# Sums of weights on VectorE instead of GpSimd, and a last product in three parts, in an attention and mixer kernel

## The chip, the cores and the metric

The kernel runs on one core of one Trainium2 chip. The metric is device time in microseconds (us) of one execution; lower is better. A few executions are more than 1.5% above the fastest of their kernel and count as slow. A profile is one execution, and its span (first to last instruction) is 1.7 to 2.0 us shorter than the device time of the same run.

In lines of the profile PE is TensorE (matrix products), PEld its loading of weights, DVE VectorE, ACT ScalarE, POOL GpSimd, and PEclk the clock granted to TensorE, in tenths. A line in order of time gives start and length in us, engine, line of the kernel, operation, output<-input, their sizes and a count; a bracket holds the engine's idle time before it and what ended that. SBUF is the on-chip memory of the tiles; TensorE writes its products to banks of another memory, PSUM.

## The reference, cut to what matters

```python
# attention, 8 batches x 8 heads x 576 positions x 64, causal, with a bias
scores = q @ k.T / 8 + minimum(bias, 0);  attn = softmax(masked scores);  x = attn @ v
# mixer on x (8 x 576 x 512)
u  = x + ((x.T @ U) @ V).T                       # low rank, along the positions
out = u + maximum(u @ w_ch1, 0) @ w_ch2          # 512 -> 2048 -> 512
```

Only the last product, hidden times `w_ch2`, matters for the change. The kernel works through the mixer in nine groups of 512 rows, as "fill" between the steps of attention. For the groups after the first it forms this product from a 2x2 block scheme with seven block products instead of eight. That scheme needs sums and differences of the blocks of `w_ch2`: B_1 = B12 - B11, B_2 = B22 - B_1, B_4 = B21 - B_2, and B_3 = B22 - B12, which takes the place of B12.

## The kernel before

The sums of the weights are made by GpSimd, three of them in one series as soon as the loads are issued, the fourth when the first group has stopped using B12:

```python
def weight_sums():
    for dst, a, b in ((B_1, B12, B11), (B_2, B22, B_1), (B_4, B21, B_2)):
        for k2 in range(0, HF, 2):                      # HF = 8
            at = (slice(None), slice(k2, k2 + 2))       # 128 x 512, bf16
            nc.gpsimd.tensor_sub(dst[at], a[at], b[at])
...
load(2); load_v(2)
weight_sums()
...
def chanmix(g, ...):
    if g > 0:
        if g == 1:                                      # fourth sum, in place
            for k2 in range(0, HF, 2): nc.gpsimd.tensor_sub(B_3[at], B22[at], B12[at])
    for nf in range(done, NF):                          # 16 chunks
        f1 = pwork(); hidden(f1, u, nf, range(4))       # TensorE
        nc.scalar.activation(hT[:, nf, :], f1, RELU)    # ScalarE
        ...
```

The causal mask of the probabilities is a VectorE instruction with two inputs in SBUF, and it stands in VectorE's queue ahead of the normalisation that frees the product banks of TensorE:

```python
nc.vector.tensor_tensor(dst, dst, keep[...].to_broadcast(...), op=ALU.min)     # mask
...
nc.vector.reciprocal(rec, po[:, :, D:D+1])                                      # values()
nc.vector.tensor_tensor(x_sb[...], po[:, :, 0:D], rec.to_broadcast(...), op=ALU.mult)
```

The end of each group, after the seventh product p7:

```python
add(U2, U2, p7); add(o22, o22, p7); send(o22, 1, 1)
p4 = bank()
for i in halves:
    product(p4, A22, B_4, i)                            # 8 matmuls 128x256 each
    if i == 0: o21 = quarter(); add_u(o21, U2, 1, 0)    # o21 = U2 + u
add(o21, o21, p4); send(o21, 1, 0)                      # 256 KB
```

The softmax here doesn't subtract the row's maximum and nothing guards it: scores larger than these inputs give would overflow.

## Time and profile before

| | kernel before |
|---|---|
| device time, three runs | 379.25, 381.78, 388.65 us (the last is slow) |
| span of the profiled run | 379.6 us |
| TensorE busy, mean granted clock | 354.7 us (93%), 0.982 |
| VectorE, ScalarE, GpSimd busy | 271.4, 204.6, 101.5 us |
| twelve GpSimd subtractions | 54.4 to 67.7 us |
| longest mask on VectorE | 12.96 us |
| longest idle time of TensorE | 12.15 us |

TensorE is the bound, so a microsecond in which it is idle or at a lower clock is a microsecond of the span, and busy time of the other engines counts only where TensorE waits for it.

### The profile page before, as it was taken

How to read it: one execution, taken by the hardware profiler on the slowest of the kernel's cores; microseconds unless marked ns; L12 is line 12 of the kernel's file. 1: busy time of each engine (PE TensorE's matmuls, PEld its weight loads, DVE VectorE, ACT ScalarE, POOL GpSimd, SP SyncE). 2: the span in 40 equal slices, each digit the busy share in tenths (PEclk: the TensorE clock that was granted, in tenths of full speed). 3: DMA queues.
4: the chain of work that ended last, by engine and by line, in shares of the span. 5: the costliest groups of instructions: out<-in, count | busy, mean ns of one | idle time of the engine just before them, and what ended most of it. 6: DMA issues, size and time to landing. Idle time of an engine off the chain costs nothing.

```text
span 379.6 us, 9369 instructions
## 1 busy us (share of the span) xinstructions
PE 354.7 (93%) x3907; PEld 249.2 (66%) x3951; DVE 271.4 (72%) x565; ACT 204.6 (54%) x309; POOL 101.5 (27%) x124
## 2 busy tenths in 40 slices
PE   7999990799999999999999999999999999999995
PEld 3675650566658866787578766886688568468474
DVE  8775779577769875898489947995698269166075
ACT  3875960275676368816881588148825550540630
POOL 8997459644404040404040404000000000000000
PEclk9999995699999999999999999999999999999999
DMA  7999999998996999799997999454012501502302
GB/s 105 168 200 205 174 178 48 60 157 109 91 106 47 112 133 140 62 74 124 139 97 75 112 151 119 53 94 100 20 38 61 124 17 57 112 2 89 79 28 85
DMA packets 147490, 37.40 MB, mean 99 GB/s; under 512 B 130616, under 2 KB 145816, under 8 KB 147448
## 3 DMA queue, kind: packets, MB, share of 16 engines
q0 software_dynamic: 104640, 18.49, 67.7%
q1 hardware_dynamic: 42808, 18.31, 25.8%
q8 instruction: 31, 0.51, 0.6%
q14 instruction: 11, 0.09, 0.1%
HBM read 37.25 MB, written 9.70 MB: 124 GB/s over the span
## 4 chain that ended last, share of the span: by engine, by line
PE 75%; DVE 12%; ACT 5%; issue 3%; DMA 3%; SPq 0%; POOL 0%; DVEq 0%; ACTq 0%; POOLq 0%
PE pwork L643 28%; PE pwork L688 20%; PE pscore L397 9%; PE pwork L457 7%; DVE hT L342 4%; PE pwork L310 3%; PE pwork L653 3%; ACT hT L789 2%; DVE uT L511 2%; DVE o_sb L702 2%; ACT pT L412 2%; DVE slot L670 2%; DMA slot<-hT 2%; DMA k_sd<-in_k_dram 1%; PE pscore L643 1%
## 5 line engine op out<-in xcount | busy, mean ns | idle before, releaser
L643 PE MATMUL pwork<-uT,w_sb 128*128 128x512 bf16 x525 | 133.6, 379 | 2.4 <-ACT hT L789 0.5
L789 ACT ACTIVATE hT<-pwork 128x512 bf16<-128x512 f32 x140 | 84.2, 605 | 61.3 <-PE pwork L643 61.1
L412 ACT ACTIVATE pT<-pscore 128x1024 bf16<-128x1024 f32 x56 | 57.1, 1029 | 69.5 <-PE pscore L397 63.7
L643 PEld LDWEIGHTS <-w_sb 128*128 128x128 bf16 x576 | 50.7, 98 | 50.0 <-issue 0.9
L397 PE MATMUL pscore<-slot 68*128 68x320 bf16 (+1 forms) x500 | 56.5, 247 | 1.0 <-DMA slot<-hT 0.8
L397 PEld LDWEIGHTS <-slot 68*128 68x128 bf16 x564 | 41.6, 98 | 18.0 <-issue 1.8
L688 PEld LDWEIGHTS <-hT 128*128 128x128 bf16 x512 | 47.7, 98 | 7.7 <-issue 0.7
L185 POOL DMA_DIRECT2D v_slot<-in_v_dram x36 | 30.3, 857 | 83.5 <-PE pwork L457 77.6
L457 PE MATMUL pwork<-v_slot,pT 128*128 128x65 bf16 x870 | 36.1, 195 | 12.4 <-DVE x_sb L467 12.1
L688 PE MATMUL pwork<-w_sb,hT 128*128 128x256 bf16 x384 | 47.5, 273 | 0.0
L342 DVE TENSOR_TENSOR pT<-pT,keep 128x512 bf16<-128x512 bf16 (+1 forms) x81 | 29.7, 366 | 22.8 <-ACT pT L412 15.9
L457 PEld LDWEIGHTS <-pT 128*128 128x128 bf16 x870 | 33.0, 99 | 17.8 <-DVE x_sb L467 12.4
L330 DVE COPY slot<-pwork 64x576 bf16<-64x576 bf16 x70 | 31.7, 453 | 4.7 <-PE pwork L310 4.1
L333 DVE COPY slot<-pwork 64x576 bf16<-64x576 bf16 x35 | 28.1, 803 | 6.1 <-PE pwork L310 4.2
L688 PE MATMUL pwork<-w_sum,slot 128*128 128x256 bf16 x256 | 31.5, 272 | 0.8 <-DVE o_sb L702 0.7
L467 DVE TENSOR_TENSOR x_sb<-pwork,rec 128x320 bf16<-128x320 f32 x64 | 31.2, 489 | 1.4
L423 ACT ACTIVATE pT<-pscore 128x1024 bf16<-128x1024 f32 x29 | 30.2, 1041 | 2.7 <-PE pscore L397 2.4
L466 DVE RECIPROCAL rec<-pwork 128x5 f32<-128x5 f32 x64 | 12.1, 190 | 23.5 <-PE pwork L457 23.2
L670 DVE TENSOR_TENSOR slot<-hT 128x1024 bf16<-128x1024 bf16 x16 | 11.0, 688 | 24.5 <-ACT hT L789 24.3
L688 PEld LDWEIGHTS <-slot 128*128 128x128 bf16 x256 | 24.1, 98 | 4.5 <-issue 1.6
L702 DVE TENSOR_TENSOR o_sb<-o_sb,pwork 128x512 f32<-128x512 f32 x32 | 21.8, 680 | 1.0 <-PE pwork L688 0.3
L111 POOL DMA_DIRECT2D q_sd<-in_q_dram x5 | 11.3, 2250 | 38.9 <-PE pwork L310 38.9
(126 smaller groups left out, 438.2 us busy)
## 6 DMA issues: line engine op xcount, KB each, us to landing
out_dram<-o_sb SPq DMA_DIRECT2D x36, 256.0 KB
w_sb<-in_moe_w_ch_dram POOLq DMA_DIRECT2D x4, 1024.0 KB, 12.4
v_slot<-in_v_dram POOLq DMA_DIRECT2D x28, 128.0 KB, 6.1
q_sd<-in_q_dram POOLq DMA_DIRECT2D x5, 576.0 KB, 12.7
k_sd<-in_k_dram POOLq DMA_DIRECT2D x5, 576.0 KB, 16.5
q_sd<-in_q_dram POOLq DMA_DIRECT2D x4, 288.0 KB, 12.4
k_sd<-in_k_dram POOLq DMA_DIRECT2D x4, 288.0 KB, 11.8
q_sd<-in_q_dram POOLq DMA_DIRECT2D x4, 144.0 KB, 5.1
```

The source lines that it names most:

```text
L185: nc.gpsimd.dma_start(out=vt[:rows_t, t, :, 0:D], in_=v[b, :, ds(t * 128, rows_t), :].rearrange("h p d -> p h d"),)
L330: copies(n, hh, par)(by_run[:, :, :, par, :], src)
L342: nc.vector.tensor_tensor(dst, dst, keep[:, :, 0:w].to_broadcast([128, n_tiles, w]), op=ALU.min)
L397: nc.tensor.matmul(dst, lhsT=slot[0:KA, hh, ds(S + j * 128, 128)], rhs=slot[0:KA, hh, lo:hi], start=True, stop=True,)
L412: nc.scalar.activation(pT[:, hh, 0:1024], near, EXP, scale=scale)
L423: nc.scalar.activation(pT[:, :, 1024:1536], mid.rearrange("p (a b) -> p a b", a=2), EXP, scale=scale)
L457: nc.tensor.matmul(po[:, i, :], lhsT=pT[:, hh, ds(place(j, i), 128)], rhs=vt[:, j, h, :], start=(j == 0), stop=(j == i), skip_group_check= ...
L467: nc.vector.tensor_tensor(x_sb[:, hp, :, ds(hh * D, D)], po[:, :, 0:D], rec.to_broadcast([128, 5, D]), op=ALU.mult,)
L643: nc.tensor.matmul(f1, lhsT=w1_sb[:, kt, ds(nf * 128, 128)], rhs=u[:, kt, :], start=(kt == 0), stop=(kt == 3),)
L688: nc.tensor.matmul(acc[:, i, :], lhsT=a[:, kt, ds(i * 128, 128)], rhs=b[:, kt, :], start=(i == 0 and kt == 0), stop=(kt == HF - 1), skip_g ...
L702: nc.vector.tensor_tensor(dst, a, b, op=ALU.add)
L789: nc.scalar.activation(hT[:, nf, :], f1, RELU)
```

## The change

Its intent is to make the sums on VectorE, in small pieces between the chunks of the second group, when GpSimd's series no longer stands in anything's way, and to let the last product of the last group leave in smaller parts. The diff, cut to its core:

```diff
     def weight_sums():
-        for dst, a, b in ((B_1, B12, B11), (B_2, B22, B_1), (B_4, B21, B_2)):
-            for k2 in range(0, HF, 2):
-                at = (slice(None), slice(k2, k2 + 2))
-                nc.gpsimd.tensor_sub(dst[at], a[at], b[at])
+        for dst, a, b in (..., (B_3, B22, B12)):
+            for k4 in range(0, HF, 4):                   # 128 x 1024
+                ...
+                nc.vector.tensor_sub(dst[at], a[at], b[at])
+                in_program_order(tc, before, [E.DVE])
+                yield
 # end of the last group
+        if g == NG - 1:
+            o21 = quarter(); add_u(o21, U2, 1, 0)
+            for i, lo, hi in ((0, 0, HD), (1, 0, 128), (1, 128, HD)):
+                ...                                      # 8 matmuls of width hi - lo
+                add(o21[:, i, lo:hi], o21[:, i, lo:hi], p4[:, 0, lo:hi])
+                (nc.sync if lo == 128 else nc.scalar).dma_start(...)
+            return
 # second group: the loop over k2 on GpSimd for B_3 goes, and
+            sums = weight_sums() if g == 1 else iter(())
             nc.scalar.activation(hT[:, nf, :], f1, RELU)
+            if g > 0:
+                next(sums, None)
 ...
     load_v(2)
-    weight_sums()
```

More of the change, by code (lines that the diff above doesn't have):

```diff
@@ L250, in weight_sums @@
     def weight_sums():
-        for dst, a, b in ((B_1, B12, B11), (B_2, B22, B_1), (B_4, B21, B_2)):
-            for k2 in range(0, HF, 2):
-                at = (slice(None), slice(k2, k2 + 2))
-                nc.gpsimd.tensor_sub(dst[at], a[at], b[at])
+        for dst, a, b in ((B_1, B12, B11), (B_2, B22, B_1), (B_4, B21, B_2), (B_3, B22, B12)):
+            for k4 in range(0, HF, 4):
+                at = (slice(None), slice(k4, k4 + 4))
+                traced = nc.cur_bb.bb.instructions
+                before = max(i for i, ins in enumerate(traced) if ins.engine == E.DVE)
+                nc.vector.tensor_sub(dst[at], a[at], b[at])
+                in_program_order(tc, before, [E.DVE])
+                yield
     nc.gpsimd.dma_start(
@@ L709, in add_u, with send @@
             )
-        def send(o, r, c, rows=slice(0, 2)):
-            n = rows.stop - rows.start
+        def send(o, r, c):
             nc.sync.dma_start(
-                out=out_flat[
-                    ds(g * 512 + r * 256 + rows.start * 128, n * 128), ds(c * HD, HD)
-                ].rearrange("(i p) d -> p i d", p=128),
-                in_=o[:, rows, :],
+                out=out_flat[ds(g * 512 + r * 256, 256), ds(c * HD, HD)].rearrange(
+                    "(i p) d -> p i d", p=128
+                ),
+                in_=o,
             )
@@ L766, in outputs_by_quarters @@
         send(o22, 1, 1)
+        if g == NG - 1:
+            o21 = quarter()
+            add_u(o21, U2, 1, 0)
+            for i, lo, hi in ((0, 0, HD), (1, 0, 128), (1, 128, HD)):
+                p4 = bank()
+                for kt in range(HF):
+                    nc.tensor.matmul(
+                        p4[:, 0, lo:hi],
+                        lhsT=A22[:, kt, ds(i * 128, 128)],
+                        rhs=B_4[:, kt, lo:hi],
+                        start=(kt == 0),
+                        stop=(kt == HF - 1),
+                    )
+                add(o21[:, i, lo:hi], o21[:, i, lo:hi], p4[:, 0, lo:hi])
+                (nc.sync if lo == 128 else nc.scalar).dma_start(
+                    out=out_flat[ds(g * 512 + 256 + i * 128, 128), lo:hi], in_=o21[:, i, lo:hi]
+                )
+            return
         p4 = bank()
@@ L781, in chanmix @@
             hT = work.tile([128, NF, 512], BF16, tag="hT", name="hT")
-            if g == 1:
-                for k2 in range(0, HF, 2):
-                    at = (slice(None), slice(k2, k2 + 2))
-                    nc.gpsimd.tensor_sub(B_3[at], B22[at], B12[at])
+            sums = weight_sums() if g == 1 else iter(())
         for nf in range(done, NF):
```

## The prediction

> **What bounds the kernel now.** I read the page first, for the shape of the span in 40 slices (9.5 us each):
>
> ```profile
> PE   7999990799999999999999999999999999999995
> DVE  8775779577769875898489947995698269166075
> POOL 8997459644404040404040404000000000000000
> PEclk9999995699999999999999999999999999999999
> ```
>
> TensorE is the bound almost everywhere (93% of the span busy), with one hole: slice 6, from 57 to 66 us, where its digit is 0 and from where its granted clock falls to 0.5 and 0.6. So I asked for the chain of waits in order of time around this hole, then for the busy times by stretch, then for GpSimd and VectorE in order of time.
>
> ```profile
> 53.32 0.81 DVE slot L333
> 54.13 0.01 issue
> 54.14 0.81 DVE slot L333
> 54.95 12.86 DVE hT L342
> 67.81 0.03 issue
> 67.84 0.21 DVE rec L466
> ```
>
> The chain's columns are start, length and what ran. It sits for 12.86 us in a single VectorE instruction at line 342, a causal mask of 128x128 bf16. The table of line 342 gives the masks on pT a range of 196 to 1229 ns, and those on hT a largest of 12956 ns. GpSimd in order of time shows what else ran then (start us, length us, engine, line, operation, how many):
>
> ```profile
> 54.38 4.48 POOL L254 TENSOR_TENSOR w_sum<-w_sb 128x512 bf16<-128x512 bf16 x4
> 58.83 8.90 POOL L254 TENSOR_TENSOR w_sum<-w_sb,w_sum 128x512 bf16<-128x512 bf16 x8
> ```
>
> VectorE over the same time, in order:
>
> ```profile
> 54.85 12.96 DVE L342 TENSOR_TENSOR hT<-hT,keep 128x128 bf16<-128x128 bf16 x1
> 67.84 0.20 DVE L466 RECIPROCAL rec<-pwork 128x5 f32<-128x5 f32 x1
> ```
>
> The twelve subtractions of the weight sums run without a gap from 54.38 to about 67.7 us (1.14 us each), and the mask that began 0.47 us after the first of them ends 0.1 us after the last. Everything behind it on VectorE waits, and TensorE with it, since its product banks are freed by the normalisation at line 467:
>
> ```profile
> 55.87 0.61 PE L397 MATMUL pscore<-slot 68*128 68x128 bf16 x6
> 68.62 1.01 PE L457 MATMUL pwork<-v_slot,pT 128*128 128x65 bf16 x15 [12.15 <-DVE x_sb L467]
> 69.84 1.49 PE L653 MATMUL pwork<-w_sb,hT 128*128 128x512 bf16 x3 [0.22 <-issue]
> ```
>
> The bracket says that TensorE was idle 12.15 us. By stretch (length; busy us of TensorE, weight load, VectorE, ScalarE, GpSimd; clock; DMA):
>
> ```profile
> 58.00:68.00 10.00, 0.00 (x0) 0.00 (x0) 9.97 (x2) 0.00 (x0) 10.00 (x10) 0.54 0.92 30
> 68.00:72.00 4.00, 3.16 (x25) 2.07 (x27) 2.14 (x7) 0.00 (x0) 4.00 (x2) 0.50 0.41 24
> 72.00:76.00 4.00, 3.94 (x64) 2.96 (x64) 2.07 (x7) 2.33 (x3) 0.15 (x1) 0.94 1.98 120
> ```
>
> After the hole TensorE goes on at half clock until about 72.3 us, then at full clock.
>
> **What the Trainium skill says.** (1) "SBUF — State Buffer", section "Who interferes with whom": a VectorE instruction with two SBUF inputs contends with a GpSimd instruction that reads SBUF, and the one that comes second blocks. The trace agrees in kind: the mask (two SBUF inputs) stood, while copies from PSUM beside the later GpSimd subtractions at 87.9 to 92.4 us kept their usual time (0.68 us for 128x512). The page speaks of holding the port "for the whole instruction"; here the mask was held over all twelve (13.0 us, not 1.1). (2) "TensorE: Matmul & The Clock Gate", section "What's actually happening": the clock halves after an idle window of about 3.4 us and recovers after a busy one. The trace agrees: 0.50 in the hole, and full again some 3.7 us after work resumed. (3) "GPSIMD Engine Reference", section "4.1 Engine selection": elementwise work with two inputs belongs on VectorE, GpSimd being about twice as slow. The trace: 1.14 us for 128x512 bf16 on GpSimd against 0.69 us for twice as much (128x1024, line 670) on VectorE.
>
> **The change part by part.**
> *Removed: the twelve GpSimd subtractions at 54 us.* TensorE's idle 12.15 us goes. Without the port being held the mask takes 0.2 us, and two reciprocals and two normalisations (0.2 + 0.5 + 0.2 + 0.5) free both banks by about 56.4 us, just when TensorE ends its scores at 56.48. So nearly all of it is won: -12.0. The half clock goes too: the work done from 68.62 to 72.84 us (lines 457, 653, 397, 457: 1.01 + 0.22 idle + 1.49 + 0.85 + 0.65 us on the chain) takes 0.45 + 0.05 + 0.65 + 0.44 + 0.45 us elsewhere at full clock, 4.2 against 2.0. A part of the difference may stay in other bubbles, so I count -1.8.
>
> *Removed: the four GpSimd subtractions of the last sum (87.91 to 92.4).* They held one mask at 91.24 for 1.23 instead of 0.2 us, but the chain runs through TensorE there and then through a ScalarE copy: 0.
>
> *Added: eight VectorE subtractions of 128x1024 bf16 in the second group, one after each of its first eight chunks.* Line 670 does this form in 0.69 us, and back to back in 0.61 (start to start), so 4.9 us of VectorE. The chunks start at 92.8 us and the first eight end at about 104. VectorE's busy time by stretches of 4 us from 92 on is 3.34, 3.72, 2.28, 2.35, 2.43: 9.3 of the 12 us to 104, and 4.9 more make 14.2. So VectorE falls about 2 to 2.5 us behind in this stage, and catches up in the next 8 us, where it has over 3 us free. TensorE is 3.82 to 4.00 of every 4 us busy there. It asks VectorE for head copies made a step ahead (those of 97.3 to 100.6 are read from 106.4 on, 5.8 us of slack) and for one of four product banks, which turn over in some 3 us. The banks are the tight part. I take half to three quarters of the backlog as lost: +1.5. GpSimd only writes descriptors there, beside which the mask at 100.48 us kept its 0.40, so no new lock.
>
> *Changed: the last product in three parts, with sends of 128, 64 and 64 KB in place of one of 256.* Before, TensorE ends its last matmul at 375.42 us, VectorE its last addition (128x512 f32, 0.69 us) at 376.40, data moves from about 377.2 to 378.2, and the span ends at 379.6. In the new form VectorE still does three additions of 0.69 us after the seventh product (they start 0.61 apart from 373.71, so the next can start at 375.5), then one of 128x256 and two of 128x128. Line 511 shows 0.41 and 0.28 us for these sizes; with starts 0.33 and 0.2 apart the last ends near 376.35. So VectorE, not TensorE, paces this end, and the last addition ends no earlier. Eight more matmuls cost TensorE 0 to 0.3 us, which is hidden behind VectorE. What is gained is data already under way: 64 KB instead of 256 remain after the last addition, 0.25 instead of 1.0 us at the rate seen. With the sharing of the engines by the earlier parts: -0.5. The end of 1.4 us, in which the sync engine waits for the transfer, stays.
>
> *Sum:* -12.0 - 1.8 + 0 + 1.5 - 0.5 = **-12.8 us**.
>
> **The rivals.** (a) *A transfer takes the place of the wait.* In the hole the DMA engines ran dry (0 GB/s from 62 to 70 us), so the kernel may then be early for its loads. Against it: the q and k of the third batch were issued by 43.3 us, land in 12 to 16 us (about 59) and are first turned at 76.0, which becomes some 62; the values of that batch, the last issued at 53.7 and landing in 8.8 us, are needed only at 94, which becomes 80. The next loads of q and k, which stood behind the subtractions until 67.7 us, go out at 54 and keep their lead. There are only some 3 us of slack on the first; I allow 2 us of new waiting at one chance in five. (b) *VectorE becomes the bound in the second group* and all 4.9 us show on TensorE: the gain falls to 9.4, the time to 371. The fraction above speaks for some of it, the free time just after against all of it. (c) *VectorE takes it wholly in its gaps:* the gain is 14.3, the time 366. (d) *The hole is not due to the subtractions* but to the mask's wait on ScalarE: against it stands that the scores' exponential before it ended at 54.1 us and that VectorE is shown busy, not waiting. That would leave the time within 1%, and I give it 3%.
>
> **Range and chances.** The three runs gave 379.25, 381.78 and 388.65 us; the last, 2.5% above the fastest, I set aside, and the profiled run took 381.42 with a span of 379.6. From a middle of 380.8: 380.8 - 12.8 = **368.0 us**. Rivals (b) with some of (a) give 372.5; (c) with a little luck in the end gives 364.5. Faster by over 2% means below some 373.5: 0.95; within 2%: 0.05; slower: 0.
>
> **What would show it.** Right: no mask above about 1 us, no clock below 0.9 after the start-up, slice 6 of TensorE at 9, the first turning of the third batch near 62 us instead of 76, eight VectorE subtractions of 0.69 us between about 79 and 91 us, and the last addition about 1 us behind the last matmul. Wrong: TensorE idle behind a DMA at 55 to 65 us (rival a), TensorE idle behind lines 330, 333 or 467 by over 2.5 us in total in the second group (rival b), or a later first transfer from the scalar queue than I allow, which would take the end's 0.5 us away.

## The result, and the profile after

| | before | changed |
|---|---|---|
| median of the runs | 381.36 us (379.25 to 388.65, 4 runs) | 367.53 us (366.95 to 368.61, 4 runs) |
| span of the profiled run | 379.6 us | 365.9 us |
| mean granted clock | 0.982 | 0.997 |

The ratio is 0.9658, with a 95% interval of 0.9609 to 0.9708: faster. (A ratio is the mean time of one kernel's fast runs over that of the other's of the same rounds, so not quite the ratio of the medians.) The median before still holds the slow run of 388.65 us; the means of the fast runs alone are 380.66 and 367.66 us, 13.0 apart. The kernel before was run again in two later calls, 11 runs each; its medians were 378.20 and 378.48 us there, and the changed kernel's repetition, in the second of them, took 366.88 us, a ratio of 0.9689. So the gain lies between 11.6 and 13.0 us, and most of the uncertainty is in the kernel before.

The page of the changed kernel, in 40 slices of 9.1 us. The hole in the row of TensorE and the dip of its clock are gone, and so is GpSimd's 9 in slice 6 (slices are counted from 0):

```profile
PE   8999999999999999999999999999999999999995
DVE  8876776679789758985699569974897188075075
POOL 8997434404040404040304022000000000000000
PEclk9999999999999999999999999999999999999998
```

VectorE at the place of the hole, in order of time. The mask that had stood for 12.96 us takes 0.20, and the normalisation follows at once:

```profile
53.90 0.20 DVE L346 TENSOR_TENSOR hT<-hT,keep 128x128 bf16<-128x128 bf16 x1
54.13 0.20 DVE L470 RECIPROCAL rec<-pwork 128x5 f32<-128x5 f32 x1
54.36 0.49 DVE L471 TENSOR_TENSOR x_sb<-pwork,rec 128x320 bf16<-128x320 f32 x1
```

TensorE there. The scores at 54.91 are those of 55.87 before; the values (now line 461) follow 0.45 us later instead of 12.75, with no idle time in brackets, and the next three matmuls of 128x512 take 0.81 us, where they took 1.49 at half clock:

```profile
54.91 0.61 PE L401 MATMUL pscore<-slot 68*128 68x128 bf16 x6
55.36 0.62 PE L461 MATMUL pwork<-v_slot,pT 128*128 128x65 bf16 x15
56.02 0.81 PE L657 MATMUL pwork<-w_sb,hT 128*128 128x512 bf16 x3
```

The busy times of the stretch that held the hole (length; busy us of TensorE, weight load, VectorE, ScalarE, GpSimd; clock; DMA). TensorE is busy for 9.77 of the 10 us, where it was for none:

```profile
58.00:68.00 10.00, 9.77 (x136) 6.63 (x137) 7.16 (x17) 6.38 (x9) 4.70 (x4) 1.00 3.64 121
```

To set the two traces against each other I use four fixed points on TensorE that every kernel here has: **a**, the four matmuls of the first group just before the hole (55.01 us before); **b**, the first chunk of the second group (92.78); **c**, the first product with a weight sum (121.68); **d**, the start of the last product (373.51). The stretches between them are far steadier than the whole time: among all the runs c to d is 251.82 to 251.86 us in eleven profiles out of fourteen.

| stretch | before | changed | difference | predicted |
|---|---|---|---|---|
| start to a | 55.01 | 54.05 | -0.96 | 0 |
| a to b: the hole and the half clock | 37.77 | 23.63 | -14.14 | -13.8 |
| b to c: second group, VectorE sums | 28.90 | 29.98 | +1.08 | +1.5 |
| c to d | 251.83 | 252.24 | +0.41 | 0 |
| d to the end: last product | 6.10 | 6.02 | -0.08 | -0.5 |
| span | 379.6 | 365.9 | -13.7 | -12.8 |

The page prints a span to 0.1 us. For every length that runs to the end of the span I take the span that the packed trace holds (379.613 and 365.917 us here).

The first and fourth lines are not of the change. The start-up (loads, and matmuls that wait for them) varies from run to run: a lies between 53.66 and 55.19 us in thirteen profiles and at 58.26 in one. In c to d the changed kernel's first look waited once for a transposing transfer, `[0.54 <-DMA xT<-x_sb]` at 190.27 us on VectorE; its repetition shows 251.82 us.

The end of a to b deserves a look at the split. From the scores to the values behind them the difference is 12.75 - 0.45 = 12.30 us, and from there to 73.11 us before (58.01 changed), where both run at full clock, it grows by another 1.84. After that it stays at 15.1 us (with the 0.96 of the start-up) up to b: so the fourth GpSimd series at 87.9 us, which stretched one mask to 1.23 us, had cost TensorE nothing.

In the second group, what VectorE waits for and what TensorE waits for can be read from the order of time. First VectorE (changed kernel), where the sums are line 256; up to 93.1 us it goes from one instruction to the next without a pause worth noting, so it runs behind:

```profile
86.27 0.67 DVE L256 TENSOR_TENSOR w_sum<-w_sb,w_sum 128x1024 bf16<-128x1024 bf16 x1
86.86 0.41 DVE L346 TENSOR_TENSOR pT<-pT,keep 128x512 bf16<-128x512 bf16 x1
87.19 0.68 DVE L256 TENSOR_TENSOR w_sum<-w_sb,w_sum 128x1024 bf16<-128x1024 bf16 x1
87.80 0.41 DVE L346 TENSOR_TENSOR pT<-pT,keep 128x512 bf16<-128x512 bf16 x1
88.13 0.68 DVE L256 TENSOR_TENSOR w_sum<-w_sb,w_sum 128x1024 bf16<-128x1024 bf16 x1
88.73 0.21 DVE L346 TENSOR_TENSOR pT<-pT,keep 128x128 bf16<-128x128 bf16 x1
88.87 0.68 DVE L256 TENSOR_TENSOR w_sb<-w_sb 128x1024 bf16<-128x1024 bf16 x1
89.58 0.26 DVE L470 RECIPROCAL rec<-pwork 128x5 f32<-128x5 f32 x2
89.81 0.89 DVE L471 TENSOR_TENSOR x_sb<-pwork,rec 128x320 bf16<-128x320 f32 x2
```

Then TensorE: it waits for line 471, the normalisation that frees a product bank and that stood behind the sums:

```profile
90.36 1.04 PE L647 MATMUL pwork<-uT,w_sb 128*128 128x512 bf16 x4 [0.60 <-DVE x_sb L471]
```

### The profile page after: what moved, and what is told of

It is laid out like the page before. It is cut to its first block, busy times and chain, and to the rows that moved or that the text cites. A ratio compares the mean times of both kernels' runs of the same rounds, so it can differ in the third digit from the quotient of the medians.

```text
span 365.9 us, 9382 instructions
## 1 busy us (share of the span) xinstructions
PE 353.9 (97%) x3915; PEld 248.5 (68%) x3959; DVE 262.0 (72%) x575; ACT 204.5 (56%) x309; POOL 83.3 (23%) x108
## 4 chain that ended last, share of the span: by engine, by line
PE 75%; DVE 12%; ACT 5%; DMA 5%; issue 3%; SPq 0%; DVEq 0%; ACTq 0%
PE pwork L647 28%; PE pwork L692 20%; PE pscore L401 9%; PE pwork L461 7%; PE pwork L314 3%; PE pwork L657 3%; DMA xT<-x_sb 3%; DVE slot L337 2%; ACT hT L807 2%; ACT pT L416 2%; DVE uT L515 2%; DVE o_sb L706 2%; DMA slot<-hT 1%; DVE slot L674 1%; PE pscore L647 1%
## 5 line engine op out<-in xcount | busy, mean ns | idle before, releaser
L692 PEld LDWEIGHTS <-hT 128*128 128x128 bf16 x496 | 46.2, 98 | 7.5 <-issue 0.7
L346 DVE TENSOR_TENSOR pT<-pT,keep 128x512 bf16<-128x512 bf16 (+1 forms) x81 | 28.6, 353 | 20.8 <-ACT pT L416 14.9
L706 DVE TENSOR_TENSOR o_sb<-o_sb,pwork 128x512 f32<-128x512 f32 (+2 forms) x34 | 21.9, 648 | 1.0 <-PE pwork L692 0.3
## 6 DMA issues: line engine op xcount, KB each, us to landing
q_sd<-in_q_dram POOLq DMA_DIRECT2D x5, 576.0 KB, 13.7
```

The source lines that it names most:

```text
L692: nc.tensor.matmul(acc[:, i, :], lhsT=a[:, kt, ds(i * 128, 128)], rhs=b[:, kt, :], start=(i == 0 and kt == 0), stop=(kt == HF - 1), skip_g ...
L706: nc.vector.tensor_tensor(dst, a, b, op=ALU.add)
```

## The experiments

All four questions are about terms of the prediction's sum: is the hole GpSimd's doing, and by what; what do the VectorE sums cost; what are the three parts worth; and can the costs be had back?

### One half of the change alone

Run sums_only: the sums on VectorE, the last product in one part.

```diff
-        if g == NG - 1:      # end in three parts
+        if False:
```

> The changed kernel with the last product in one part again, so only the sums are moved. If the three parts are worth the 0.5 us of the prediction, this takes 0.5 us more than the changed kernel (about 368.0 against 367.5 us), and 0.966 to 0.968 of the kernel before. If, as the profile of the changed kernel suggests, they are worth 0.1 us, no difference can be seen (ratio about 0.966). From the start of the last product to the end of the span: 6.1 us, as in the kernel before, against 6.0 in three parts.

Measured: 367.64 us median (366.58 to 372.1, 6 runs, one of them slow), ratio to the kernel before 0.9695 (0.9649 to 0.974). From d to the end 6.09 us. So nearly all of the gain is in the sums, and against the 6.02 us of three parts the end is 0.07 us longer.

Run tail_only: the kernel before, sums on GpSimd at their old place, with the last product in three parts.

```diff
+        if g == NG - 1:      # end in three parts, as in the changed kernel
+            ...
+            return
         p4 = bank()
```

> The kernel before with the last product in three parts, the sums still on GpSimd. Theory (all of the gain is in the sums): within 0.5 us of the kernel before, ratio 0.998 to 1.001, the mask again stands for about 13 us beside the twelve subtractions, and TensorE is idle 12 us. If the end mattered more than thought, the ratio is below 0.997.

Measured: 379.45 us median (377.68 to 385.25, 6 runs, one slow), ratio 1.0026 (0.9968 to 1.0084): the same. From d to the end 6.02 us. The profile of this run brought something not expected. GpSimd's series began at 54.37 us, within 0.01 us of where it began in the kernel before (the load that GpSimd issues just ahead of it waits for a transfer); but start-up had been 1.35 us quicker (a at 53.66), and the 128x128 mask was through before the series came. The *next* mask was caught, for 11.75 us:

```profile
53.51 0.20 DVE L342 TENSOR_TENSOR hT<-hT,keep 128x128 bf16<-128x128 bf16 x1
...
55.84 0.49 DVE L467 TENSOR_TENSOR x_sb<-pwork,rec 128x320 bf16<-128x320 f32 x1
56.25 11.75 DVE L342 TENSOR_TENSOR pT<-pT,keep 128x512 bf16<-128x512 bf16 x1
67.93 0.18 DVE L466 RECIPROCAL rec<-pwork 128x5 f32<-128x5 f32 x1
```

TensorE had been given more work by then, so it was idle for less (the bracket says 9.60 us where the kernel before shows 12.15), and a to b took 35.46 us instead of 37.77:

```profile
68.69 0.29 PE L397 MATMUL pwork<-slot 68*128 68x64 bf16 x2 [9.60 <-DVE x_sb L467]
```

So what the hole costs depends on which mask meets the series. That would explain why the runs of the kernel before spread from 377.3 to 382 us; but only two of its kind were profiled, and this is an inference.

### What in GpSimd's work holds the mask

Run writes_only: the changed kernel, with GpSimd memsets where the subtractions stood, for nearly the same length of time (12.6 against 13.4 us). It separates "GpSimd reads SBUF" from "GpSimd is busy, and its loads are held back".

```diff
+    for dst in (B_1, B_2, B_4):                       # at the old place of weight_sums()
+        for k2 in range(0, HF, 2):
+            for _ in range(2): nc.gpsimd.memset(dst[at], 0.0)
```

> The changed kernel, with 24 GpSimd memsets of 128x512 bf16 put where the twelve subtractions stood, into the same buffers (the VectorE sums overwrite them later, so the result stays right). GpSimd is as busy at that place and its later descriptor work is held back in the same way, but it reads nothing. Theory (the mask waits for GpSimd's reads): no mask over 0.5 us, TensorE without a hole, the time as the changed kernel's within 1 us. Rival (any GpSimd work there blocks VectorE, or the loads held behind it make the hole): a mask as long as the memsets (some 12 us) or a wait for a transfer of several us, and 375 us or more.

Measured: 24 memsets from 56.21 us, 12.60 us in all, and no mask beside them is slower than usual:

```profile
56.21 12.60 POOL L264 MEMSET w_sum<- 128x512 bf16 x24
```

```profile
58.11 0.20 DVE L353 TENSOR_TENSOR hT<-hT,keep 128x128 bf16<-128x128 bf16 x1
60.85 0.41 DVE L353 TENSOR_TENSOR pT<-pT,keep 128x512 bf16<-128x512 bf16 x1
62.62 0.42 DVE L353 TENSOR_TENSOR pT<-pT,keep 128x512 bf16<-128x512 bf16 x1
```

From a to b 23.64 us, as in the changed kernel (23.63). The time of this one look was 371.91 us, above the expected 1 us; the whole excess lies before a (58.26 us, with a dip of the clock in slices 1 and 2) and 0.5 us at the end, so it isn't of this stage. The rival falls: a GpSimd that is busy with writes, and loads held back behind it, make no hole.

Run one_input: twelve GpSimd copies (one SBUF input) at that place.

```diff
+            nc.gpsimd.tensor_copy(dst[at], B11[at])
```

> The changed kernel, with twelve GpSimd copies of 128x512 bf16 (one SBUF input) where the twelve subtractions stood, overwritten later by the VectorE sums. Theory (one read by GpSimd is enough to hold a mask with two SBUF inputs): the mask there stands until the end of the copies, say 6 to 12 us, and the time grows by about as much over the changed kernel's. Rival (only two-input GpSimd work blocks): no mask over 0.5 us and the time of the changed kernel.

Measured: the copies ran from 53.92 us for 6.71 us, and the mask stood for 6.38:

```profile
53.92 6.71 POOL L263 COPY w_sum<-w_sb 128x512 bf16<-128x512 bf16 x12
```

```profile
53.77 6.38 DVE L352 TENSOR_TENSOR hT<-hT,keep 128x128 bf16<-128x128 bf16 x1
```

From a to b 30.67 us, 7.0 more than the changed kernel. One input read by GpSimd is enough. (The mask's record starts 0.15 us before the first copy, but the VectorE instruction ahead of it is on record until 53.89, so the two records don't say which came first.) Both runs agree with what the Trainium skill states in "SBUF — State Buffer", section "Who interferes with whom": a VectorE instruction with two SBUF inputs contends with a GpSimd one that reads SBUF, not with one that only writes.

Run gaps: the kernel before, with a memset between every two subtractions.

```diff
                 nc.gpsimd.tensor_sub(dst[at], a[at], b[at])
+                nc.gpsimd.memset(gap, 0.0)             # spare tile, 128x512
```

> The kernel before with a GpSimd memset of 128x512 bf16 into a spare tile (some 0.5 us, writes only) after each of the twelve subtractions, so that GpSimd's reads have gaps. Theory A (a mask gets in as soon as GpSimd reads nothing for a moment): no mask over about 1.3 us, TensorE's idle time there at most 2 to 3 us, and the stretch from the fixed point before the hole to the first chunk of the second group 24 to 28 us instead of 37.8. Theory B (a mask is held until GpSimd's whole run of tensor work is over): a mask of some 18 to 20 us, and that stretch over 40 us.

Measured: 386.76 us in one look. My theory A fell, and B held but for the last memset: the half microsecond of write-only work between the subtractions lets no mask in. The mask stood for 23 of the 24 instructions of the series:

```profile
53.95 18.71 DVE L344 TENSOR_TENSOR hT<-hT,keep 128x128 bf16<-128x128 bf16 x1
```

```profile
71.44 1.14 POOL L255 TENSOR_TENSOR w_sum<-w_sb,w_sum 128x512 bf16<-128x512 bf16 x1
72.53 0.52 POOL L256 MEMSET gap<- 128x512 bf16 x1
```

Its end, at 72.66 us, falls together with the end of the last subtraction (72.58), not of the memset behind it (73.05). So theory B had the length right, but what the mask waited out was the last read. TensorE was idle for 17.91 us, and a to b took 44.00.

Run last_on_gpsimd: the changed kernel with only the in-place sum, four subtractions, on GpSimd, behind the third chunk of the second group.

```diff
-        for dst, a, b in (..., (B_3, B22, B12)):
+        for dst, a, b in (...):
 ...
                 next(sums, None)
+                if g == 1 and nf == 2:
+                    for k2 in range(0, HF, 2): nc.gpsimd.tensor_sub(B_3[at], B22[at], B12[at])
```

> The changed kernel with the in-place sum (four subtractions of 128x512) on GpSimd again, put behind the third chunk of the second group; the other six sums stay on VectorE. Theory: masks and VectorE sums have two SBUF inputs, so those that fall beside the four subtractions (4.6 us) are held, one for up to 4.6 us, and the stretch from the first chunk to the first product with a sum is longer than the 30.0 us with all sums on VectorE, by 1 to 4 us. Rival (four subtractions are too short to matter, as they seemed to be in the kernel before): 29.3 to 29.8 us, less than with all eight on VectorE.

Both expectations missed: b to c took 30.03 us, the same as with all sums on VectorE. The third subtraction waited 0.80 us for VectorE before it began, and beside it one VectorE sum was held, for 1.29 us instead of 0.68; it ended at 84.21, when the third was over (83.67) and the fourth had begun:

```profile
82.92 1.29 DVE L256 TENSOR_TENSOR w_sum<-w_sb,w_sum 128x1024 bf16<-128x1024 bf16 x1
```

```profile
83.63 1.60 POOL L813 TENSOR_TENSOR w_sb<-w_sb 128x512 bf16<-128x512 bf16 x1
```

Now it was GpSimd's fourth that was held (1.60 instead of 1.15 us). So VectorE can get in between two GpSimd subtractions, and wasn't let in during the series at 54 us. VectorE is spared two sums here (1.4 us) and held for 0.6, and TensorE gains nothing by it.

Run spread: the sums on GpSimd, one subtraction after each of the sixteen chunks, each behind a small copy that was to wait for its chunk. In the trace only three of the sixteen copies show a wait for ScalarE, which writes the chunks (10.00, 0.86 and 0.50 us); GpSimd ran behind for the others, so they stood queued back to back after all.

```diff
-            for k4 in range(0, HF, 4):
-                nc.vector.tensor_sub(dst[at], a[at], b[at])
+            for k2 in range(0, HF, 2):
+                nc.gpsimd.tensor_sub(dst[at], a[at], b[at]); yield
 ...
+                if g == 1: nc.gpsimd.tensor_copy(gap, hT[:, nf, 0:2])    # waits for the chunk
                 next(sums, None)
```

> The changed kernel with the sums on GpSimd again, but one subtraction of 128x512 after each of the sixteen chunks of the second group, each behind a tiny GpSimd copy that has to wait for that chunk, so that no two stand queued back to back. Theory C (a VectorE instruction is held over many GpSimd instructions only where these are queued without a wait): no VectorE instruction over 1.9 us (its own time and one subtraction), and the stretch from the first chunk of the second group to its first product with a sum 29 to 31 us, near the 30.0 with all sums on VectorE. Rival D (the hold does not depend on the queue): single masks of 3 us and more and a stretch over 32 us.

The first half of theory C's forecast came true, though its condition was not met: no VectorE instruction in the second group is longer than 1.78 us, that is, its own time and one subtraction. The second half missed: b to c took 33.50 us, because the holds now fell on the sums of the hidden layer (line 673, otherwise 0.69 us), which come close together:

```profile
97.22 1.65 DVE L673 TENSOR_TENSOR slot<-hT 128x1024 bf16<-128x1024 bf16 x1
98.78 0.18 DVE L469 RECIPROCAL rec<-pwork 128x5 f32<-128x5 f32 x1
98.90 1.66 DVE L673 TENSOR_TENSOR slot<-slot,hT 128x1024 bf16<-128x1024 bf16 x1
100.48 0.48 DVE L470 TENSOR_TENSOR x_sb<-pwork,rec 128x320 bf16<-128x320 f32 x1
```

and TensorE waited twice for the normalisation behind them, 2.09 us at 101.01 and 2.47 at 111.46. Another wait of 2.15 us, at 122.83 behind line 514, and a half clock just after it (0.50 from 124 to 127 us) make up what c to d grew by (255.45); I did not follow that wait further. So spreading the subtractions shortens each hold to one of them, but TensorE still loses more by it (33.50 us) than with the sums on VectorE (30.00). What decides whether a hold ends with one GpSimd instruction or lasts over a series stays open. Waits that GpSimd has to sit out aren't it: between the third and fourth subtraction of last_on_gpsimd there was none, and none between the subtraction and the next copy here, and VectorE got in; this copy, otherwise 0.18 us, was then the one that was held:

```profile
97.14 1.17 POOL L254 TENSOR_TENSOR w_sum<-w_sb,w_sum 128x512 bf16<-128x512 bf16 x1
98.26 0.65 POOL L809 COPY gap<-hT 128x2 bf16<-128x2 bf16 x1
```

### What the VectorE sums cost

Run no_sums: a wrong result; the VectorE sums are left out, and GpSimd memsets fill the buffers with zeros.

```diff
-            sums = weight_sums() if g == 1 else iter(())
+            sums = iter(())
```

> The changed kernel without the eight VectorE sums (twelve GpSimd memsets fill the buffers with zeros at the old place, the in-place sum is not made): a wrong result on purpose. Theory (the eight sums cost TensorE 1.1 us in the second group): from the first chunk of the second group to its first product with a sum 28.9 us as in the kernel before, against 30.0 with the sums. Rival (the stretch is longer because this group comes earlier, beside other transfers): 29.5 us or more.

Measured: b to c 28.90 us, exactly that of the kernel before, with the 252 us behind it unchanged (251.84). The eight sums cost 30.00 - 28.90 = 1.1 us of the 4.9 us that VectorE spends on them.

### Having both costs back

Run changed_again is the yardstick.

> The changed kernel itself, as the yardstick for the other runs of this call: 367.5 us within 1 us, ratio about 0.966 to 0.970.

366.88 us median (366.64 to 367.88, 6 runs), ratio 0.9689 (0.9655 to 0.9723); b to c 30.00, d to the end 6.01.

Run early_sums: six of the eight sums are made beside the outputs of the first group.

```diff
+    all_sums, early = weight_sums(), [0]
 ...
             for _ in outputs(f2, hT, i, ...):         # first group
+                if early[0] < 6: early[0] += 1; next(all_sums)
                 yield
```

> The changed kernel, with six of the eight VectorE sums put beside the outputs of the first group, where VectorE has more gaps, and only the two of the in-place sum left in the second group. Theory (the 1.1 us lost between the first chunk of the second group and its first product with a sum is VectorE's backlog): that stretch falls from 30.0 to 28.9 to 29.2 us, and no new loss over 0.3 us appears before it, so 0.7 to 1.1 us less than the changed kernel in the same call. Rival (the loss has another cause, or only moves to the earlier stage): within 0.3 us of the changed kernel.

Measured: b to c 29.23 us, a to b 23.64 (unchanged), so 0.77 us is won and nothing is lost in the earlier stage: VectorE had the gaps there. The median is 366.44 us (366.23 to 368.39, 6 runs), 0.44 below the yardstick's, which is less than the stage shows but within the spread of runs.

Run early_end: one addition of the last group is made while the seventh product is under way.

```diff
             product(p7, A_3, B_3, i)
             if i == 0:
                 add_u(o22, o22, 1, 1)
+                if g == NG - 1: o21 = quarter(); add_u(o21, U2, 1, 0)
-        add(U2, U2, p7)
         add(o22, o22, p7); send(o22, 1, 1)
+        if g == NG - 1: add(o21, o21, p7)
```

> The changed kernel, with one addition of the last group (the quarter's running sum plus u) made while the seventh product is still under way, so that VectorE has two additions of 0.69 us instead of three between the seventh product and the parts of the last. Theory (VectorE, not TensorE or the transfer, paces the end, which is why three parts were worth only 0.1 us): the stretch from the start of the last product to the end of the span falls from 6.0 to 5.4 to 5.5 us, and the time by 0.5 us. Rival (the transfer's fixed time paces it): it stays at 5.9 to 6.0.

Measured: d to the end 5.41 us instead of 6.01, as expected from two additions in place of three: VectorE paces the end. The median is 366.85 us (366.15 to 373.96, 6 runs, one slow), so by the whole time alone it could not be told from the yardstick. The end of VectorE's work in the yardstick, and then in early_end:

```profile
360.70 0.68 DVE L706 TENSOR_TENSOR o_sb<-U,u_sd 128x512 f32<-128x512 f32 x1
361.49 0.82 DVE L706 TENSOR_TENSOR o_sb<-o_sb,pwork 128x256 f32<-128x256 f32 x3
```

```profile
359.49 2.21 DVE L706 TENSOR_TENSOR o_sb<-o_sb,pwork 128x512 f32<-128x512 f32 x5 [0.28 <-PE pwork L692]
```

The last product starts at 359.29 us in both, so the last addition ends 3.02 us after it in the yardstick and 2.41 after it in early_end.

Run both: the two edits together.

> Both of these edits at once. Theory: the two add up, 1.2 to 1.6 us less than the changed kernel of this call, about 366 us. Rival: no difference beyond the spread of runs, 0.3 us.

Measured: 365.88 us median (365.38 to 366.96, 6 runs), ratio to the kernel before 0.9661 (0.9624 to 0.9699). The mean of its six runs is 365.97 us, that of the yardstick's six 367.11: 1.1 us less, a little under the 1.2 to 1.6 expected. b to c is 29.23 us and d to the end 5.42. This version is the fastest, by 0.3% over the changed kernel; its slowest run (366.96) lies above the yardstick's three fastest, so the stages carry the proof better than the times.

## Why the prediction was right

The predicted 368.0 us stands against 367.53 measured, and each term of the sum can be measured by itself.

**The hole (-12.0) and the half clock (-1.8).** Right: -12.30 and -1.84. The experiments show the cause that had been argued from the profile alone: reads by GpSimd hold a mask with two SBUF inputs (one_input, gaps), writes alone do not (writes_only). Rival (d), a mask that waits for ScalarE, is out. Rival (a), a transfer in place of the wait, did not come: a to b is 23.63 us with a single TensorE wait of 0.3 us in it, which was there before. The first turning of the third batch moved from 76.02 to 60.93 us. One reading behind it was loose: "the trace agrees" with an idle window of some 3.4 us holds for the kind and not for the number. The clock fell to half 2.3 us after the last matmul had ended (58.8 and 56.48 us), and after 1.5, 2.3 and 4.3 us in one_input, gaps and tail_only; it was full again 2.8 to 5.0 us after work resumed.

**The fourth GpSimd series (0).** Right: the distance between the two traces does not change over it. The 0.68 us that the prediction gives for copies from PSUM beside this series belong to copies just before and after it (87.24 and 92.86 us); what ran beside it were casts from PSUM, and they too kept their time (the two at 89.51 took 1.29 us together, as do the same two in the changed kernel at 74.40, with GpSimd idle).

**The VectorE sums (+1.5).** The right mechanism, a size too large by 0.4: 1.1 us (no_sums). TensorE lost it where the prediction had looked for it, at the product banks behind line 467 (now 471; two waits of 0.8 us in all, against one of 0.2 before). VectorE caught up in the gaps behind, so rival (b), all 4.9 us, is out, and so is rival (c), none.

**The last product in three parts (-0.5).** The right mechanism and the wrong size: 0.08 us. One part takes 6.09 to 6.11 us from d to the end in the three profiles that have it, three parts 6.01 to 6.02 in eight of nine (6.48 in writes_only; early_end and both change the end again). The prediction had VectorE's last addition "end no earlier" and put the gain into "data already under way". The last addition ended 2.89 us after d before (376.40 - 373.51) and 3.02 after it in the changed kernel, 0.13 later. The prediction had it at 2.84 (376.35), with the first addition of the last product possible at 375.5. But that one starts 0.79 us after the addition before it, whose result it reads, and not 0.61; the kernel before shows the same, and so do the yardstick's lines above (360.70 and 361.49):

```profile
374.92 0.69 DVE L702 TENSOR_TENSOR o_sb<-U,u_sd 128x512 f32<-128x512 f32 x1
375.71 0.69 DVE L702 TENSOR_TENSOR o_sb<-o_sb,pwork 128x512 f32<-128x512 f32 x1
```

From the last addition to the end of the span it was 3.21 us before and 3.00 after: with 64 KB instead of 256 in the last transfer this stretch is 0.22 us shorter, not 0.75 as the rate alone gives, nor the 0.5 that the prediction allowed. The 0.13 lost takes back more than half of it. That VectorE paces the end was right, and early_end, which takes one addition away from it, gained the 0.6 us.

**The time before.** The prediction started from 380.8 us. Later the kernel before took 378.2 to 378.5, and the gain was 11.6 us (medians) instead of 13.0 (fast runs). Run tail_only shows how its hole can be 2.3 us smaller. So a part of the agreement in the gain is luck with the kernel before; the changed kernel's own time was 367.5, 367.6 (without the three parts) and 366.9.

## What to carry to other kernels

Work on GpSimd that reads SBUF is not free just because GpSimd is idle: look in the trace for a VectorE instruction with two SBUF inputs that lasts as long as a GpSimd series, and count what TensorE waits behind it, with the slow clock after. The same work on VectorE, cut into pieces and put where VectorE has gaps, cost 1.1 us of TensorE's time for 4.9 us of VectorE's, and 0.3 where the gaps were better chosen. At the end of a kernel, first find which engine paces the last results; cutting the last product into parts won next to nothing while three additions stood ahead of it on VectorE.

## What the Trainium skill lacked or had wrong

- "SBUF — State Buffer", section "SBUF: two separate sides", has the port pair held for the whole instruction, and the other engine blocked until then. Here a VectorE mask was held over whole series of GpSimd instructions: 12.96 us over twelve subtractions of 1.14, 6.38 us over copies of 0.56, and 18.71 us over twelve subtractions with a write-only memset of 0.52 between each two. In other places it was held for one instruction at most (1.29 and 1.65 us in all). The page speaks of deep queues that would have to be drained to share, but doesn't say when the port is handed over between queued instructions, and these runs don't settle it.
- "GPSIMD Engine Reference", section "4.1 Engine selection", gives GpSimd's lower rate, about half, as the reason not to use it for two-input elementwise work. Here it was 3.3 times slower per element (1.14 us for 128x512 against 0.69 for 128x1024), and the rate was not what cost time: what it did to VectorE and, through it, to TensorE was, 14.1 us for 13.4 us of GpSimd work that nothing waited for. The page names the contention in another place, its key points, but not in this row.
- No page that I found gives what cutting a last store into parts saves, beyond times for a single transfer. With 64 KB instead of 256 KB in the last transfer, the time from the last addition to the end of the span was 0.22 us shorter, 3.21 to 3.00.
